# Turning q and k by 32 by 32 blocks on VectorE and transfers, with sums moved to GpSimd and to an adding transfer

## The chip, the cores and the metric

The kernel runs on one core of a Trainium2 chip. A core has TensorE (matmuls, with weight loads beside them), VectorE (DVE), ScalarE (ACT), GpSimd (POOL) and SyncE (SP, which here only issues transfers); ScalarE and GpSimd can issue transfers too. The metric is the device time of one execution in microseconds (us), less is better.

## The reference

Hashed attention over 4 batches, 8 heads, 768 tokens and 64 channels is followed by a two-layer network with a leaky activation.

```python
q_bits = (np.einsum('bhsd,dk->bhsk', q, proj) > 0)      # 6 bits; k_bits likewise
mask = q_bucket[:, :, :, None] == k_bucket[:, :, None, :]   # the bits as one number
scores = np.where(mask, scale * np.matmul(q, k.transpose(0, 1, 3, 2)), -1e9)
attn = softmax(scores)                                   # exp, sum, divide
x = (attn @ v), heads side by side                       # 3072 x 512
h = x @ w_in                                             # 512 x 2048
g = np.maximum(h, 0.0) + alpha * np.minimum(h, 0.0)
out = g @ w_out                                          # 2048 x 512
```

w_in and w_out come as 64-bit floats and are rounded to 32 bits in the kernel.

## The kernel before

The program tries `fast_path`; a flag that it computes decides whether `general_path` runs as well, and in the profiled execution it does not. `fast_path` has two parts: attention, and the two matrix products of the network, each of them done with seven half-size products in place of eight.

**Attention** works on 16 pairs of heads (`pi`), one after another. Of a pair, tokens lie on the partitions as they come from memory: token 6p + c is at partition p, slot c of the tile `nat`, whose row holds 64 channels of each of the two heads. Scores need channels on the partitions. `turn(pi, name)` makes them: six TensorE transposes of 128 by 128 into a PSUM tile, then one ScalarE copy into `tr` (q is scaled by a small constant there). The column order of `tr` is slot by slot. `hash_bits` multiplies `tr` with the projection and takes signs on ScalarE into `kb`; from there six small transfers on the SP queue bring the bits of q into `qb` and part of k's bits into place. `scores` goes through twelve cells (six tiles of 128 keys by two groups of 384 queries). A cell has, for each of the two heads, a bf16 matmul on the bits and an fp32 one on `tr`, which add up in PSUM, and one exponential on ScalarE over both heads into `pts[kc]`. `attend` multiplies with v, `totals` sums over keys with a matrix of ones, and `divide` finishes on VectorE and stores `x_s`.

The sum over six key tiles that `totals` needs is made on VectorE: `add_first` (tiles 0 and 1), `add_third` (tile 2), `add_last` (tiles 3 to 5, two additions), `add_total`. `magnitude` squares q and k in place on ScalarE, for the flag.

**Beside it**, two pieces of the weights are rounded in each iteration: `load_weight` (SP queue), `weight_abs` (two ScalarE passes), and `weight_clamp`, `weight_parts`, `weight_sum` on VectorE. For each of four groups of w_in, `weight_group` queues four more additions and a store into `w_in_s`; `weight_sums(2)` issues up to two of these additions an iteration.

**Order.** Most engine instructions go through `do`, which pins them behind what was written before on the same engine. Transfers without `do` are ordered by a planner that estimates when they are ready. PSUM has three two-bank tiles for scores, turns and sums. A tile's `tag` with `bufs=n` means that n tiles of this tag exist and that the next one waits until all users of the oldest are done.

The order of one iteration, cut to what matters here:

```python
scores(pi, ...); divide(pi - 1, weight_begin)   # with add_first(pi) inside
weight_sum(i); weight_group(i); load_weight(i + 3); weight_clamp(i + 1)
add_third(pi); add_last(pi); weight_parts(i + 1); weight_sum(i + 1)
weight_group(i + 1); load_weight(i + 4); add_total(pi); weight_sums(2)
hash_bits(pi + 1); turn(pi + 2, "q"); turn(pi + 2, "k")
attend(pi); totals(pi); weight_abs(i + 2); load(pi + 2, "v")
magnitude(pi, "q"); load(pi + 3, "q"); magnitude(pi, "k"); load(pi + 3, "k")
weight_abs(i + 3)
```

Pairs 0 and 1 are turned ahead of the loop.

Of the kernel before, what the change touches and what calls it, by code (L numbers as in the profile page):

```python
# [8 lines left out]
F32 = mybir.dt.float32  # L9
# [3 lines left out]
AF = mybir.ActivationFunctionType  # L13
ALU = mybir.AluOpType
# [393 lines left out]
def fast_path(  # L408
# [12 lines left out]
    nc = tc.nc  # L421
    P = 128
    B, H, S, D = q.shape
# [5 lines left out]
    NC = S // P  # L429
    NK = DM // P  # L430
    NF = DFF // P
    CH = 3
    NCH = NC // CH
    CW = CH * P
    HW2 = CW // 2
    SCALE = float(D) ** -0.5
    DOWN = 2.0 ** -20
# [5 lines left out]
    do = tc.keep_in_program_order  # L443
    PE, DVE, ACT, POOL = nc.tensor, nc.vector, nc.scalar, nc.gpsimd
# [32 lines left out]

    pts = [pool.tile([P, NCH, 2, CW + 1], F32, name=f"pt{i}", bufs=1) for i in range(NC)]

    nat, tr, bits = {}, {}, {}  # L480
    accp, accd, av, vsum, sums = {}, {}, {}, {}, {}

# [10 lines left out]
    def load_part(pi, name, cs, queue):  # L493
        b, hp = pairs[pi]
        src = {"q": q, "k": k}[name]
        if cs.start == 0:
            nat[name, pi] = pool.tile([P, NC, 2, D], F32, name=f"{name}n{pi}", tag=f"{name}n", bufs=3)
        for s in range(2):
            queue.dma_start(nat[name, pi][:, cs, s], src[b, 2 * hp + s].rearrange("(p c) d -> p c d", c=NC)[:, cs])

# [32 lines left out]
    def setup_alpha():  # L533
        ps = two_banks("alps")[:, 0, :NF]
        do(PE.transpose(ps, alpha16, ident[:NF, :NF]))
        do(DVE.tensor_copy(alpha, ps))
# [91 lines left out]
    def weight_group(i):  # L628

        i = order[i]  # L630
        if i >= HW:
            n, m = divmod(i - HW, 2)
            if m == 1:
                nc.sync.dma_start(w_out_r[:, :, n].rearrange("m p d -> p m d"), wst[HW + n])
            return
        n, m = divmod(i, 4)
        if m < 3:
            return
        w = wst[n]

        def one(to, a, op, c):
            do(DVE.tensor_tensor(w[:, to], w[:, a], w[:, c], op=op))

        def store():
            c, kk = divmod(n, 2)
            for ii in range(4):
                nc.sync.dma_start(w_in_s[4 * c + ii][:, :, kk], w[:, :, ii])


        for x in ((3, 5, 2), (5, 0, 5), (4, 3, 0), (6, 1, 4)):  # L650
            sums_due.append((one, (x[0], x[1], ALU.subtract, x[2])))
        sums_due.append((store, ()))
# [14 lines left out]
    def turn(pi, name, halves=BOTH, engine=None):  # L667
# [10 lines left out]
        else:  # L678
            do(ACT.activation(dst, ps[:, halves, :CW], AF.Copy, scale=DOWN if name == "q" else 1.0))

    def magnitude(pi, name):

        t = nat[name, pi].rearrange("p c h d -> p (c h d)")
        n = "qk".index(name)
        do(ACT.activation(t, t, AF.Square, accum_out=mags[:, n, pi : pi + 1]))

    def hash_bits(pi, halves=BOTH, engine=None):

        if halves.start == 0:
            bits["q", pi] = qbs[pi % 2]
            kb = pool.tile([P, 3 * CW], BF16, name=f"kb{pi}", tag="kb", bufs=1)
            bits["k", pi] = kb[:, :S]
            bits["raw", pi] = kb.rearrange("p (a w) -> p a w", w=CW)
        ps = {"k": two_banks(f"hs{pi}")}
        ps["q"] = psum_av.tile([P, 2, 512], F32, name=f"hsq{pi}", tag="av") if engine is DVE else ps["k"]
        for half in range(halves.start, halves.stop):
            for name in "qk" if engine is DVE else "kq":
                for s in range(2):  # L700
                    r, c = D * s, D * (s ^ half) + 32 * "kq".index(name)

                    for t, c in [("k", c)] + ([("q", c ^ D)] if engine is DVE and name == "q" else []):
                        do(PE.matmul(
                            ps[t][c : c + 32, half if t == "k" or engine is not DVE else 0, :CW], wh[r : r + D],
                            tr[name, pi][r : r + D, half * CW : (half + 1) * CW], start=True, stop=True,
                        ))
        if engine is None:
            raw = bits["raw", pi]
            do(ACT.activation(raw[:, 0:3:2], ps["k"][:, :, :CW], AF.Sign, bias=hb))  # L710
            for half in range(2):
                for s in range(2):
                    c = D * (s ^ half)
                    cols = slice(half * CW, (half + 1) * CW)
                    nc.sync.dma_start(bits["q", pi][D * s : D * s + 32, cols], raw[c + 32 : c + 64, 2 * half])
                    if half:
                        nc.sync.dma_start(bits["k", pi][D * s : D * s + D, cols], raw[c : c + D, 2])
            return
        for half in range(halves.start, halves.stop):
            cols = slice(half * CW, (half + 1) * CW)  # L720
            for s in range(2):
                c = D * (s ^ half ^ (engine is DVE)) + 32
                do(ACT.activation(
                    bits["q", pi][D * s : D * s + 32, cols], ps["q"][c : c + 32, 0 if engine is DVE else half, :CW], AF.Sign, bias=hb[c : c + 32],
                ))

            for to, c, n in [(0, 0, P)] if half == 0 else [(0, D, D), (D, 0, D)]:
                dst, src = bits["k", pi][to : to + n, cols], ps["k"][c : c + n, half, :CW]
                do(DVE.tensor_scalar(
                    dst, src, hb_k[c : c + n, 0:1], hb_k[c : c + n, 1:2], op0=ALU.is_gt, op1=ALU.subtract,  # L730
                ))


    def scores(pi, cells):
        for kc, g in cells:
            sc = two_banks(f"sc{pi}_{kc}_{g}")
            ks = slice(kc * P, (kc + 1) * P)
            qs = slice(g * CW, (g + 1) * CW)
            for what, first in ((bits, True), (tr, False)):
                for s in range(2):  # L740
                    r = slice(D * s, D * s + D)
                    do(PE.matmul(  # L742
                        sc[:, s, :CW], what["k", pi][r, ks], what["q", pi][r, qs], start=first, stop=not first,
                    ))
            do(ACT.activation(pts[kc][:, g, :, :CW], sc[:, :, :CW], AF.Exp, scale=SCALE / DOWN))  # L745


    def p(kc):
        return pts[kc].rearrange("p g s w -> p (g s) w")[:, :, :CW]

    def add_first(pi):
        accp[pi] = pool.tile([P, 2 * NCH, CW], F32, name=f"accp{pi}", tag="accp", bufs=1)
        do(DVE.tensor_tensor(accp[pi], p(0), p(1), op=ALU.add))  # L753

    def add_last(pi):
        accd[pi] = pool.tile([P, 2 * NCH, CW], F32, name=f"accd{pi}", tag="accd", bufs=1)
# [1 line left out]
        do(DVE.tensor_tensor(accd[pi], accd[pi], p(5), op=ALU.add))  # L758

    def add_third(pi):  # L760
        do(DVE.tensor_tensor(accp[pi], accp[pi], p(2), op=ALU.add))  # L761

    def add_total(pi):
        do(DVE.tensor_tensor(accd[pi], accd[pi], accp[pi], op=ALU.add))  # L764
# [375 lines left out]
    for pi in range(NPAIR):  # L1140
        i = 2 * pi

        def weight_begin():
            weight_clamp(i)
            weight_parts(i)
            add_first(pi)

        scores(pi, [c for c in CELLS if pi or c not in ahead])
        if pi:
            divide(pi - 1, weight_begin)  # L1150
        else:
            add_first(pi)
        weight_sum(i)
        weight_group(i)
        load_weight(i + 3)
        if pi == 0:
            weight_abs(1, DVE)
        weight_clamp(i + 1)
        add_third(pi)
        add_last(pi)  # L1160
        weight_parts(i + 1)
        weight_sum(i + 1)
        weight_group(i + 1)
        load_weight(i + 4)
        add_total(pi)
        weight_sums(2)
        if pi + 1 < NPAIR:
            hash_bits(pi + 1)
        if pi + 2 < NPAIR:
            turn(pi + 2, "q")  # L1170
            turn(pi + 2, "k")
        attend(pi)
        if pi + 1 == NPAIR:
            now = ff1(0, 0)
            now.step(1)
        totals(pi)
        if pi + 1 == NPAIR:
            now.step(5)
            divide(pi)
        else:  # L1180
            weight_abs(i + 2)
        if pi + 2 < NPAIR:
            load(pi + 2, "v")
        if pi in (9, 11, 15):
            load_w((9, 11, 15).index(pi))
        if pi in (9, 10, 12):
            load_x(0, *{9: (0,), 10: (2, 3), 12: (1,)}[pi])
        if 11 <= pi < 14 or pi == 15:
            sum_x(0, min(pi - 11, 3), DVE)
        if pi == 1:  # L1190
            setup_alpha()
        for name in "qk":
            magnitude(pi, name)
            if pi + 3 < NPAIR:
                load(pi + 3, name)
        if pi + 1 < NPAIR:
            weight_abs(i + 3)
# [97 lines left out]
```

## Time and profile before

| | us |
|---|---|
| three runs, median (lowest to highest) | 897.62 (896.51 to 897.95) |
| the profiled execution, its own time | 897.64 |
| span of its profile | 895.8 |
| TensorE busy | 884.2 (99%) |
| VectorE busy | 746.8 (83%) |
| ScalarE busy | 379.5 (42%) |
| GpSimd busy | 14.4 (2%) |
| attention: last store of `x_s` issued at | 347.3 |

The span is what the profiler saw of the core's instructions. Busy shares are means over the whole span; the two parts use the engines differently (from 60 to 310 us ScalarE is busy for 192.9 of 250 us, VectorE for 217.7, TensorE for 247.9). A group's line gives the source line, the engine, what is written from what, the count, then the busy time, the mean of one in ns, and the idle time ahead of it with what ended it. In the timeline a line begins with start and length in us. "SPq" is the issue of a transfer by SP.

### The profile page before, as it was taken

The numbers are of one execution on the slowest core, as the hardware profiler recorded it, in microseconds if no ns is written. First come the engines' busy times: TensorE is split into PE (matmuls) and PEld (weight loads), VectorE is DVE, ScalarE is ACT, GpSimd is POOL, SyncE is SP. The second block draws the span as 40 slices with busy tenths as digits, with TensorE's granted clock in tenths as the row PEclk, the third lists the DMA queues.
The fourth block names the chain that finished last, engine by engine and source line by source line (L and its number), as shares of the span: only waits on it lengthen the run. The fifth ranks groups of instructions, "written<-read, shape, count | busy, mean of one in ns | idle before, by whom it ended". The sixth has DMA issues, their size and how long they took to land.

```text
span 895.8 us, 15331 instructions
## 1 busy us (share of the span) xinstructions
PE 884.2 (99%) x5886; PEld 598.5 (67%) x5886; DVE 746.8 (83%) x1266; ACT 379.5 (42%) x668; POOL 14.4 (2%) x30
## 2 busy tenths in 40 slices
PE   9999999999999999999999999999999999999996
PEld 4544545555555545557997557997557998556996
DVE  5888888888989887899989678988668989768996
ACT  7877777788877762222112222112222111222111
POOL 1000000000000001120000000000000000000000
PEclk9999999999999999999999999999999999999998
DMA  8444575575685625587333435343525242430242
GB/s 235 139 143 129 151 232 153 149 229 173 204 281 163 202 74 185 181 296 289 141 113 107 163 111 166 107 147 88 178 88 192 95 159 80 157 116 0 95 143 72
DMA packets 126177, 137.22 MB, mean 153 GB/s; under 512 B 78976, under 2 KB 110224, under 8 KB 122512
## 3 DMA queue, kind: packets, MB, share of 16 engines
q1 hardware_dynamic: 121376, 126.59, 44.9%
q0 software_dynamic: 2304, 8.39, 2.6%
q10 hardware_dynamic: 2416, 1.18, 0.5%
q8 instruction: 48, 0.79, 0.3%
q14 instruction: 33, 0.27, 0.1%
HBM read 104.87 MB, written 28.31 MB: 149 GB/s over the span
## 4 chain that ended last, share of the span: by engine, by line
PE 84%; DVE 9%; issue 3%; ACT 2%; DMA 2%; SPq 0%; DVEq 0%; ACTq 0%
PE sc L742 12%; PE av L775 10%; PE f_0a L875 2%; PE z_4a L875 2%; PE z_7a L875 2%; PE z_3a L875 2%; PE z_6a L875 2%; PE z_5a L875 2%; PE f_4a L875 2%; PE f_3a L875 2%; PE f_2a L875 2%; PE f_1a L875 2%; PE z_2a L875 2%; PE f_5a L875 2%; DMA qb<-kb 2%
## 5 line engine op out<-in xcount | busy, mean ns | idle before, releaser
L745 ACT ACTIVATE pt<-sc 128x768 f32<-128x768 f32 x192 | 154.8, 812 | 53.5 <-PE sc L742 53.2
L742 PE MATMUL sc<-qT,kT 64*128 64x384 f32 x768 | 155.8, 483 | 0.0
L775 PE MATMUL av<-pt,vn 128*32 128x385 f32 (+1 forms) x1536 | 127.4, 486 | 0.0
L742 PEld LDWEIGHTS sc<-qT,kT 64*128 64x128 f32 x768 | 70.0, 187 | 40.9 <-issue 40.7
L775 PEld LDWEIGHTS av<-pt,vn 128*32 128x32 f32 x1536 | 48.7, 109 | 71.1 <-issue 70.5
L928 DVE TENSOR_TENSOR g<-g,g 128x384 f32<-128x384 f32 x128 | 68.4, 555 | 2.2
L742 PE MATMUL sc<-qb,kb 64*128 64x384 bf16 x384 | 66.5, 323 | 2.4 <-DMA qb<-kb 2.1
L992 DVE TENSOR_TENSOR gs<-g,gs 128x768 f32<-128x768 f32 x56 | 53.3, 952 | 1.0
L992 DVE TENSOR_TENSOR gs<-g 128x768 f32<-128x768 f32 x56 | 53.3, 951 | 0.0
L984 DVE TENSOR_TENSOR ws<-wl 128x512 f32<-128x512 f32 x56 | 38.5, 687 | 17.5 <-DMA wl<-w_out_s 15.9
L753 DVE TENSOR_TENSOR accp<-pt,pt 128x1536 f32<-128x1536 f32 x16 | 28.1, 1759 | 17.5 <-ACT pt L745 17.5
L924 DVE SCALAR_TENSOR_TENSOR g<-h,alpha 128x384 f32<-128x384 f32 x32 | 19.7, 616 | 25.1 <-ACT h L917 25.1
L742 PEld LDWEIGHTS <-kb 64*128 64x128 bf16 x384 | 20.9, 94 | 25.9 <-issue 4.3
L580 ACT ACTIVATE wr<-raw 128x512 int32<-128x512 uint32 x32 | 22.8, 712 | 17.2 <-issue 16.0
L758 DVE TENSOR_TENSOR accd<-accd,pt 128x1536 f32<-128x1536 f32 x16 | 28.1, 1759 | 2.0 <-ACT wr L580 0.5
L761 DVE TENSOR_TENSOR accp<-accp,pt 128x1536 f32<-128x1536 f32 x16 | 28.0, 1753 | 0.0
L757 DVE TENSOR_TENSOR accd<-pt,pt 128x1536 f32<-128x1536 f32 x16 | 28.0, 1752 | 0.0
L764 DVE TENSOR_TENSOR accd<-accd,accp 128x1536 f32<-128x1536 f32 x16 | 28.0, 1751 | 0.0
L805 DVE STREAM_TRANSPOSE st<-sm 128x192 f32<-128x192 f32 x32 | 10.3, 361 | 16.9 <-PE sm L789 16.9
L875 PE MATMUL f_0a<-x,wi 128*128 128x384 f32 x64 | 23.5, 489 | 0.0
L875 PE MATMUL f_4a<-x,wi 128*128 128x384 f32 x64 | 23.3, 486 | 0.0
L875 PE MATMUL f_1a<-x,wi 128*128 128x384 f32 x64 | 23.3, 486 | 0.0
(348 smaller groups left out, 1732.1 us busy)
## 6 DMA issues: line engine op xcount, KB each, us to landing
wi<-w_in_s SPq DMA_DIRECT2D x32, 896.0 KB, 4.7
wl<-w_out_s SPq DMA_DIRECT2D x16, 1024.0 KB, 4.8
wl<-w_out_r SPq DMA_DIRECT2D x12, 1024.0 KB, 4.9
raw<-in_moe_w_out_dram SPq DMA_DIRECT2D x16, 512.0 KB, 3.9
raw<-in_moe_w_in_dram SPq DMA_DIRECT2D x16, 512.0 KB, 4.0
w_in_s<-wsi SPq DMA_DIRECT2D x16, 448.0 KB, 5.8
vn<-in_v_dram SPq DMA_DIRECT2D x16, 384.0 KB, 4.2
x_s<-x SPq DMA_DIRECT2D x16, 384.0 KB, 2.8
```

The costliest lines, as they stand in the source:

```text
L742: do(PE.matmul(sc[:, s, :CW], what["k", pi][r, ks], what["q", pi][r, qs], start=first, stop=not first,))
L745: do(ACT.activation(pts[kc][:, g, :, :CW], sc[:, :, :CW], AF.Exp, scale=SCALE / DOWN))
L753: do(DVE.tensor_tensor(accp[pi], p(0), p(1), op=ALU.add))
L757: do(DVE.tensor_tensor(accd[pi], p(3), p(4), op=ALU.add))
L758: do(DVE.tensor_tensor(accd[pi], accd[pi], p(5), op=ALU.add))
L761: do(DVE.tensor_tensor(accp[pi], accp[pi], p(2), op=ALU.add))
L764: do(DVE.tensor_tensor(accd[pi], accd[pi], accp[pi], op=ALU.add))
L775: do(PE.matmul(av[pi][D * s + t : D * s + t + 32, g, :w], nat["v", pi][:, s, kc * D + t : kc * D + t + 32], pts[kc][:, g, s, :w], start=(k ...
L875: do(PE.matmul(self.ps[bank], self.left(left, k), self.right(right, k), start=start and k == 0, stop=k == self.nk - 1, skip_group_check=no ...
L928: do(DVE.tensor_tensor(new_g(b, to)[:, i], g_m[b, x][:, i], g_m[b, y][:, i], op=ALU.subtract))
L984: do(DVE.tensor_tensor(t, w2[b, n, x], w2[b, n, y], op=op))
L992: do(DVE.tensor_tensor(t, g2[b, n, x], g2[b, n, y], op=ALU.subtract))
```

## The change

- q and k of pairs 2 to 15 are no longer turned by `turn`. `turn_blocks` lets VectorE transpose all 32 by 32 blocks of `nat` at once into a tile of tag "tb" (one buffer for both names), and sixteen transfers on the SP queue, each of 32 partitions by 192 floats, put the blocks at their place in `tr`. k comes first, then q. The columns of `tr` are then in token order; `columns` picks a tile's columns out of `tr` and of the bits with a step of six elements. `scale_q` scales q on ScalarE.
- `nat` has two buffers instead of three for q and k, and `magnitude` runs two pairs ahead.
- The six transfers of `hash_bits` go to ScalarE's queue and are pinned in its order.
- The four additions of a w_in group run on GpSimd.
- From pair 1 on, half of `add_third` is done by an adding transfer on GpSimd's queue, issued in `add_first`.

```diff
-            nat[name, pi] = pool.tile(..., tag=f"{name}n", bufs=3)
+            nat[name, pi] = pool.tile(..., tag=f"{name}n", bufs=2 if name in WITH_DVE else 3)
...
-            do(DVE.tensor_tensor(w[:, to], w[:, a], w[:, c], op=op))
+            do(POOL.tensor_tensor(w[:, to], w[:, a], w[:, c], op=op))
...
+    def turn_blocks(pi, name):
+        t = pool.tile([P, 4, 32, NC], F32, name=f"{name}B{pi}", tag="tb", bufs=1)
+        do(DVE.transpose(t.rearrange("p b i c -> p b c i"), nat[name, pi].rearrange("p c h (e d) -> p (h e) c d", d=32)))
+        w = NC * 32
+        tr[name, pi] = dst = pool.tile([P, S], F32, name=f"{name}T{pi}", tag=f"{name}T")
+        for a in range(4):
+            for b in range(4):
+                nc.sync.dma_start(
+                    dst[32 * b : 32 * b + 32, a * w : (a + 1) * w],
+                    t[32 * a : 32 * a + 32, b].rearrange("p i c -> p (i c)"),
+                )
+        by_blocks.add((name, pi))
+
+    def scale_q(pi):
+        if ("q", pi) in by_blocks:
+            do(ACT.activation(tr["q", pi], tr["q", pi], AF.Copy, scale=DOWN))
+
+    def columns(what, name, pi, r, c0, c1):
+        t = what[name, pi][r]
+        if (name, pi) not in by_blocks:
+            return t[:, c0 * P : c1 * P]
+        t = t.rearrange("p (t c) -> p c t", c=NC)[:, c0:c1]
+        return t[:, 0] if c1 - c0 == 1 else t
...
-                    nc.sync.dma_start(bits["q", pi][D * s : D * s + 32, cols], raw[c + 32 : c + 64, 2 * half])
+                    do(nc.scalar.dma_start(bits["q", pi][D * s : D * s + 32, cols], raw[c + 32 : c + 64, 2 * half]))
                     if half:
-                        nc.sync.dma_start(bits["k", pi][D * s : D * s + D, cols], raw[c : c + D, 2])
+                        do(nc.scalar.dma_start(bits["k", pi][D * s : D * s + D, cols], raw[c : c + D, 2]))
...
-                        sc[:, s, :CW], what["k", pi][r, ks], what["q", pi][r, qs], start=first, stop=not first,
+                        sc[:, s, :CW], columns(what, "k", pi, r, kc, kc + 1),
+                        columns(what, "q", pi, r, CH * g, CH * (g + 1)), start=first, stop=not first,
...
         do(DVE.tensor_tensor(accp[pi], p(0), p(1), op=ALU.add))
+        if pi:
+            nc.gpsimd.dma_start(accp[pi][:, 2:], p(2)[:, 2:], accum_op=ALU.add)
...
-        do(DVE.tensor_tensor(accp[pi], accp[pi], p(2), op=ALU.add))
+        n = 2 if pi else 4
+        do(DVE.tensor_tensor(accp[pi][:, :n], accp[pi][:, :n], p(2)[:, :n], op=ALU.add))
...
             hash_bits(pi + 1)
+        if pi == 0:
+            for name in WITH_DVE:
+                magnitude(0, name)
         if pi + 2 < NPAIR:
-            turn(pi + 2, "q")
-            turn(pi + 2, "k")
+            turn_blocks(pi + 2, "k")
+            turn_blocks(pi + 2, "q")
         attend(pi)
...
+        scale_q(pi + 2)
         for name in "qk":
-            magnitude(pi, name)
+            for n in [1, 2] if pi == 0 and name in WITH_DVE else [pi + 2 * (name in WITH_DVE)]:
+                if n < NPAIR:
+                    magnitude(n, name)
```

More of the change, by code (lines that the diff above doesn't have):

```diff
@@ L478, in fast_path @@
     pts = [pool.tile([P, NCH, 2, CW + 1], F32, name=f"pt{i}", bufs=1) for i in range(NC)]
+    WITH_DVE = "qk"
     nat, tr, bits = {}, {}, {}
@@ L496, in load_part @@
         if cs.start == 0:
-            nat[name, pi] = pool.tile([P, NC, 2, D], F32, name=f"{name}n{pi}", tag=f"{name}n", bufs=3)
+            nat[name, pi] = pool.tile([P, NC, 2, D], F32, name=f"{name}n{pi}", tag=f"{name}n", bufs=2 if name in WITH_DVE else 3)
         for s in range(2):
@@ L679, in turn @@
             do(ACT.activation(dst, ps[:, halves, :CW], AF.Copy, scale=DOWN if name == "q" else 1.0))
+    def turn_blocks(pi, name):
[10 more added lines that the diff above has]
+        by_blocks.add((name, pi))
+    by_blocks = set()
+    def scale_q(pi):
[7 more added lines that the diff above has]
+        return t[:, 0] if c1 - c0 == 1 else t
     def magnitude(pi, name):
@@ L736, in scores @@
             sc = two_banks(f"sc{pi}_{kc}_{g}")
-            ks = slice(kc * P, (kc + 1) * P)
-            qs = slice(g * CW, (g + 1) * CW)
             for what, first in ((bits, True), (tr, False)):
```

## The prediction

> **What bounds the kernel now.** I read the page's busy shares and clock first, then the groups by line, then the timeline of single engines over one head pair, since a share says nothing of order.
>
> ```profile
> PE 884.2 (99%) x5886; PEld 598.5 (67%) x5886; DVE 746.8 (83%) x1266; ACT 379.5 (42%) x668; POOL 14.4 (2%) x30
> ...
> PEclk9999999999999999999999999999999999999998
> ```
>
> TensorE is busy throughout at full clock, so every microsecond taken off it alone could be won. The stage that the change touches is the attention part, sixteen pairs up to about 350 us. Its groups of TensorE turns:
>
> ```profile
> L674 PE MATMUL tp_q<-ident,qn 128*128 128x128 f32 x96 | 14.5, 287 | 0.0
> L674 PE MATMUL tp_k<-ident,kn 128*128 128x128 f32 x96 | 13.6, 277 | 0.0
> ```
>
> Matmuls overlap, so I take the cost from the timeline: the first tp_q starts at 167.82 and the next stage (av) at 169.28, thus 1.46 us a pair. Next ScalarE's timeline, one pair:
>
> ```profile
> 168.05 0.90 ACT L710 ACTIVATE kb<-hs,hb 128x768 bf16<-128x768 f32 x1
> ...
> 174.26 0.73 ACT L580 ACTIVATE wr<-raw 128x512 int32<-128x512 uint32 x1 [1.09 <-issue]
> 174.88 0.70 ACT L584 ACTIVATE wx<-raw 128x512 f32<-128x512 f32 x1
> 178.92 9.70 ACT L745 ACTIVATE pt<-sc 128x768 f32<-128x768 f32 x12 [3.34 <-PE sc L742]
> 188.65 0.90 ACT L710 ACTIVATE kb<-hs,hb 128x768 bf16<-128x768 f32 x1
> ```
>
> The Sign (L710) follows a pair's last exponential at once; its starts mark the pairs. From the first (22.59) to the fifteenth (314.27) are 14 intervals in 291.7 us, **20.83 us a pair**. ScalarE waits 3.34 us for scores before the next pair's twelve exponentials. VectorE and SP in the same pair:
>
> ```profile
> 170.63 1.76 DVE L758 TENSOR_TENSOR accd<-accd,pt 128x1536 f32<-128x1536 f32 x1
> ...
> 174.10 1.75 DVE L764 TENSOR_TENSOR accd<-accd,accp 128x1536 f32<-128x1536 f32 x1
> ```
> ```profile
> 168.97 1.85 SPq L715 DMA_DIRECT2D qb<-kb  x3
> ```
> ```profile
> L715 SPq DMA_DIRECT2D qb<-kb x60: 511/585/1282, 23.6 to 320.9; - x60
> ...
> DMA to landing us min/median/max: 1.8/2.4/5.4
> ```
>
> VectorE is only 7.85 us behind: the last exponential ends at 168.00, add_total (L764) at 175.85. SP takes 0.62 us from issue to issue (three in 1.85) for a transfer of 32 rows of 768 bytes that lands after 2.4 us. The new transfers have just this shape.
>
> [...]
>
> **The change part by part.** Fourteen pairs (2 to 15) are turned the new way, in iterations 0 to 13.
>
> *Removed.* TensorE 1.46 us a pair, in all 20.4 us; ScalarE's two copies, 0.81 us each; VectorE's sixteen w_in adds of 0.69 us, 11.0 us in all, and half of each later add_third, 0.88 us.
>
> *Added on a serial path.* This decides. All engine instructions concerned are pinned in program order, so a wait holds everything behind it.
> 1. k's block turn stands on VectorE behind add_total, and q's directly behind k's. Both write a tile of tag "tb" with bufs=1, so q's turn waits until all sixteen of k's transfers have read it. Behind it wait divide and the next pair's sums.
> 2. scale_q stands on ScalarE behind weight_abs and ahead of the squares, weight_abs(i+3) and **the next pair's exponentials**. It waits for q's sixteen transfers.
> 3. add_total needs this pair's last exponential. So one pair's exponentials, both rounds of transfers, and the next pair's exponentials form a chain.
>
> From one last exponential to the next:
> - to the end of add_total: 7.85 - 0.88 = 6.97
> - k's turn: 0.97 (L816, a transpose of as many elements)
> - k's transfers: 15 x 0.62 + 2.4 = 11.7
> - q's turn and transfers: 0.97 + 11.7
> - scale_q: 0.85 (as an L685 square)
> - both squares: 1.79 (150.14 to 151.93)
> - weight_abs(i+3): 1.31 (153.02 to 154.33)
> - twelve exponentials: 9.70
>
> Sum **46.0 us**, against 20.83. Outside the transfers it is already 22.6.
>
> *Unknowns on it.* Restart: TensorE finishes its work some 9 us after E (E: a pair's last exponential) and then idles over 20 us[...]. A scores cell takes 0.81 us, as long as an exponential; [...] I take 1.5. Strided scores: k and q are now read in steps of 24 bytes, their bits 12. Bounds: nothing, or a cell at half speed, 0.8 us x 12 = 9.7 us a pair. In the timeline a cell's fp32 matmuls start 0.16 us after its bf16 ones and fill the other 0.64 in two passes, half the bf16 pace, so I expect the bf16 pass alone to suffer, 0.08 of its 0.16 us: 1.0 us a pair. The strided weight loads overlap matmuls (a step of 8 bytes costs 196 against 190 ns in the z products); I count them in that bound. Together **48.5 us a pair**.
>
> *Moved, with cover.* Six bit transfers go to ScalarE: 6 x 0.6 = 3.6 us behind the Sign, inside its new wait for scale_q, so nothing; uncovered they'd be 3.6 us a pair. SP gains 32 x 0.62 = 19.8 us and loses 3.7; its other transfers (q, k, v, raw, x_s, w_in_s) take some 6 us, so 26 of 48.5 us: not the bound, though whatever is queued between the new ones delays them, 0 to 5 us a pair. In four iterations it can be w_in_s's four stores (4.5 us). The w_in adds run on GpSimd while VectorE waits: nothing[...]. The adding transfer starts after add_first (about E - 4.7), passes POOL's queue, and at the 6.8 us of POOL's own loads lands at E + 2, before add_total at E + 5.2: nothing; if its tile is tracked whole, add_third waits some 3 us. Shorter buffers for q and k cost once: pair 2's load waits for magnitude(0), behind the Sign (0.9), six issues (3.6) and two squares (1.8), so it starts at E + 6.3 and lands at E + 11.9, 4.9 late; iteration 0 has two squares more, 1.8. Together 6.7 us.
>
> *Sum.* 14 x 48.5 = 679.0, less 291.7: +387.3. With 6.7 and 1.0 for pair 15's strided scores: +395. The profiled execution took 897.64 (span 895.8), the median of three runs is 897.62: **1292 us**. TensorE's 20.4 us are saved where nobody waits.
>
> **The rivals.** *Cheaper issue.* SP issues a plain full-width load in 0.33 us and the output's pieces in about 0.47. At 0.35 a round is 4 us shorter, the pair 8.1: 1292 - 14 x 8.1 = 1179. For it speaks that L715's cost is not explained by its bytes; against it, 60 equal transfers never went under 0.51. *Strided reads at half speed.* A cell goes from 0.81 to 1.6 us and TensorE paces the exponentials: 9.7 for 1.0, 1292 + 14 x 8.7 = 1414. *Only VectorE is held.* If scale_q did not stand before the exponentials, VectorE alone would set the pair: busy 217.7 of 250 us, or 18.1 a pair, less 0.9 and 0.8 plus 1.9 for the turns, plus one round of 11.7 and hand-offs: 30.2, so 897.6 + 14 x 9.4 = 1029. The order in the code speaks against it. *Faster.* Turns hidden altogether, TensorE still the bound: 897.6 - 20.4 = 877. It decides below 20.83 us a pair; with the sum's 22.6 us outside the transfers even free transfers miss that, so ScalarE and VectorE would both have to run past the waits. That the turns don't leave TensorE is excluded by the diff.
>
> **How the numbers follow.** Both rounds on the path near 0.6 us an issue: 0.68, own range 1210 to 1380. Cheaper issue 0.11, strided reads at half speed 0.12, VectorE alone 0.06, turns hidden 0.02, a tie by accident 0.01. A measurement of this kernel can tell about 0.2% (1.8 us) from no change. The range of 8 in 10 runs from the cheap end to the strided end: 1180 to 1420. Faster 0.02, same 0.01, slower 0.97.
>
> **What would show it.** Right: exponentials of pairs 1 to 14 behind a wait of some 27 us for scale_q, this behind q's transfers; some 12 us of idle VectorE before each q turn; Sign starts about 48 us apart; attention ending near 745 us, later stages as long as now; low clock digits in it. Wrong: q's turn close behind k's, exponentials ahead of scale_q, or issues of 0.3 us.

## The result, and the profile after

| | us |
|---|---|
| before, median of the runs beside it | 897.68 (896.51 to 897.95) |
| after, median of four runs | 1374.15 (1373.63 to 1375.16) |
| ratio after to before | 1.531 (95% interval 1.529 to 1.534) |
| span of the profile after | 1372.6 |
| last store of `x_s` issued at | 823.6 (before: 347.3) |

The kernel takes half as long again. The last store of `x_s` moved by 476.3 us, which is the whole difference: from there to the end of the span it is 549.0 us after and 548.5 before. So only the attention part is to be read.

From the page of after come first the busy shares and the granted clock, then the share of each engine in the chain of work that ended last, then four groups (out<-in, count | busy us, mean ns of one | idle us before it, and what ended it):

```profile
PE 1050.5 (77%) x5718; PEld 638.6 (47%) x5718; DVE 778.0 (57%) x1278; ACT 365.9 (27%) x654; POOL 58.6 (4%) x61
...
PEclk9588687786786886876867899999999999999999
...
PE 57%; SPq 18%; DVE 9%; ACT 5%; DMA 5%; issue 2%; ACTq 1%; DVEq 0%
...
L768 PE MATMUL sc<-qb,kb 64*128 64x384 bf16 x384 | 131.6, 646 | 312.4 <-ACT pt L772 184.8
L768 PE MATMUL sc<-qT,kT 64*128 64x384 f32 x768 | 285.8, 815 | 0.0
...
L684 DVE STREAM_TRANSPOSE qB<-qn 128x768 f32<-128x768 f32 x14 | 21.5, 1534 | 165.3 <-DMA kT<-kB 165.3
L699 ACT ACTIVATE qT<-qT 128x768 f32<-128x768 f32 x14 | 11.8, 842 | 358.3 <-DMA qT<-qB 358.3
```

No engine is near full, and the issue of transfers by SP (SPq) is 18% of the chain, 247 us. The two waits of the prediction are there, fourteen times each: q's turn waits 165.3 / 14 = 11.8 us for k's transfers, `scale_q` (L699) 358.3 / 14 = 25.6 us for q's. TensorE has 168 instructions fewer and is busy 166 us **longer**: a matmul of the scores takes 815 ns (fp32) and 646 ns (bf16), where the page of before has 483 and 323:

```profile
L742 PE MATMUL sc<-qT,kT 64*128 64x384 f32 x768 | 155.8, 483 | 0.0
L742 PE MATMUL sc<-qb,kb 64*128 64x384 bf16 x384 | 66.5, 323 | 2.4 <-DMA qb<-kb 2.1
```

One pair, in ScalarE's timeline (start us, length us; in brackets the idle time before it and what ended it):

```profile
293.14 0.90 ACT L738 ACTIVATE kb<-hs,hb 128x768 bf16<-128x768 f32 x1
...
324.11 0.84 ACT L699 ACTIVATE qT<-qT 128x768 f32<-128x768 f32 x1 [24.24 <-DMA qT<-qB]
...
327.60 2.19 ACT L772 ACTIVATE pt<-sc 128x768 f32<-128x768 f32 x3
330.53 0.81 ACT L772 ACTIVATE pt<-sc 128x768 f32<-128x768 f32 x1 [0.74 <-PE sc L768]
332.39 0.81 ACT L772 ACTIVATE pt<-sc 128x768 f32<-128x768 f32 x1 [1.06 <-PE sc L768]
...
346.39 0.90 ACT L738 ACTIVATE kb<-hs,hb 128x768 bf16<-128x768 f32 x1
```

VectorE and SP in the same pair:

```profile
296.52 1.75 DVE L794 TENSOR_TENSOR accd<-accd,accp 128x1536 f32<-128x1536 f32 x1
298.19 1.62 DVE L684 STREAM_TRANSPOSE kB<-kn 128x768 f32<-128x768 f32 x1
311.30 1.53 DVE L684 STREAM_TRANSPOSE qB<-qn 128x768 f32<-128x768 f32 x1 [11.48 <-DMA kT<-kB]
```
```profile
299.88 10.08 SPq L689 DMA_DIRECT2D kT<-kB  x16
...
312.85 10.02 SPq L689 DMA_DIRECT2D qT<-qB  x16
```

Read from top to bottom by time, this is one thread: last exponential (ends 293.02), add_total, k's turn, sixteen issues, landing, q's turn, sixteen issues, landing, `scale_q`, squares, `weight_abs`, the next exponentials. Each step begins where the one before it ends. The Sign starts lie 53.2 to 55.0 us apart, in the mean of 14 intervals (22.04 to 778.27) **54.0 us**; the prediction had 48.5. What it didn't have is the last stretch: behind the third exponential each one waits for TensorE, and they come every 1.87 us instead of every 0.81.

### The profile page after: what moved, and what is told of

It reads as the page before. It is cut to its first block, busy times and chain, and to the rows that moved or that the text cites. A ratio compares the mean times of both kernels' runs of the same rounds, so it can differ in the third digit from the quotient of the medians.

```text
span 1372.6 us, 15577 instructions
## 1 busy us (share of the span) xinstructions
PE 1050.5 (77%) x5718; PEld 638.6 (47%) x5718; DVE 778.0 (57%) x1278; ACT 365.9 (27%) x654; POOL 58.6 (4%) x61
## 4 chain that ended last, share of the span: by engine, by line
PE 57%; SPq 18%; DVE 9%; ACT 5%; DMA 5%; issue 2%; ACTq 1%; DVEq 0%
SPq L689 18%; PE sc L768 18%; DMA qT<-qB 2%; DMA kT<-kB 2%; DVE accd L794 2%; DVE kB L684 2%; DVE qB L684 2%; PE z_4a L905 2%; PE f_0a L905 2%; PE z_3a L905 2%; PE z_5a L905 2%; PE z_7a L905 2%; PE z_6a L905 2%; PE f_3a L905 2%; PE f_1a L905 2%
## 5 line engine op out<-in xcount | busy, mean ns | idle before, releaser
L768 PE MATMUL sc<-qb,kb 64*128 64x384 bf16 x384 | 131.6, 646 | 312.4 <-ACT pt L772 184.8
L768 PE MATMUL sc<-qT,kT 64*128 64x384 f32 x768 | 285.8, 815 | 0.0
L768 PEld LDWEIGHTS <-kb 64*128 64x128 bf16 x384 | 29.6, 120 | 397.8 <-issue 260.4
L772 ACT ACTIVATE pt<-sc 128x768 f32<-128x768 f32 x192 | 152.0, 809 | 136.6 <-PE sc L768 136.6
L768 PEld LDWEIGHTS sc<-qT,kT 64*128 64x128 f32 x768 | 121.9, 293 | 100.7 <-issue 100.3
L684 DVE STREAM_TRANSPOSE qB<-qn 128x768 f32<-128x768 f32 x14 | 21.5, 1534 | 165.3 <-DMA kT<-kB 165.3
L699 ACT ACTIVATE qT<-qT 128x768 f32<-128x768 f32 x14 | 11.8, 842 | 358.3 <-DMA qT<-qB 358.3
L782 POOL DMA_DIRECT2D accp<-pt x15 | 18.1, 1209 | 725.9 <-DVE x L852 380.9
L643 POOL TENSOR_TENSOR wsi<-wsi 128x512 f32<-128x512 f32 x16 | 27.9, 1746 | 27.4 <-DVE wsi L625 26.7
L684 DVE STREAM_TRANSPOSE kB<-kn 128x768 f32<-128x768 f32 x14 | 22.8, 1627 | 5.2 <-DMA kn<-in_k_dram 5.2
```

The source lines that it names most:

```text
L684: do(DVE.transpose(t.rearrange("p b i c -> p b c i"), nat[name, pi].rearrange("p c h (e d) -> p (h e) c d", d=32)))
L768: do(PE.matmul(sc[:, s, :CW], columns(what, "k", pi, r, kc, kc + 1), columns(what, "q", pi, r, CH * g, CH * (g + 1)), start=first, stop=no ...
```

## The experiments

Each variant was timed beside the kernel before. "Sign spacing" is the time between the starts of two Signs, a pair's period. e1 to e4 ask for the price of each link of the chain, e8 splits the price of the stepped reads, and the others ask what is left once the chain is broken or the turns stay on TensorE.

### e1_strided: the stepped reads alone

The kernel before, with TensorE's turns; only the column order of `tr` is changed for pairs 2 to 15.

```diff
-            do(ACT.activation(dst, ps[:, halves, :CW], AF.Copy, scale=...))
+            dst = tr[name, pi].rearrange("p (t h c) -> p h c t", h=NCH, c=CH)[:, halves] if pi > 1 else dst
+            src = ps[:, halves, :CW].rearrange("p h (c t) -> p h c t", c=CH) if pi > 1 else ps[:, halves, :CW]
+            do(ACT.activation(dst, src, AF.Copy, scale=...))
...
-                        sc[:, s, :CW], what["k", pi][r, ks], what["q", pi][r, qs], start=first, stop=not first,
+                        sc[:, s, :CW], columns(what, "k", pi, r, kc, kc + 1),
+                        columns(what, "q", pi, r, CH * g, CH * (g + 1)), start=first, stop=not first,
```

> The kernel before, with one thing added: for pairs 2 to 15 ScalarE's copy writes the turned q and k in token order, so that scores reads both, and their bits, in steps of six elements, as after does. TensorE still turns; no new transfer or wait. Theory (the strided reads are a cost of their own, in the new profile a cell takes 1.87 us at half and at full clock): 12 x (1.87 - 0.81) = 12.7 us a pair, 14 pairs, 897.7 + 178 = 1075 us. Rival (the long cells of after come from TensorE's restarts at half clock): cells stay at 0.81 us and the time at 898 to 905 us.

Measured: **1072.83 us**, ratio 1.195 (1.193 to 1.197). Its score groups:

```profile
L750 PE MATMUL sc<-qT,kT 64*128 64x384 f32 x768 | 290.0, 807 | 0.0
...
L750 PE MATMUL sc<-qb,kb 64*128 64x384 bf16 x384 | 137.4, 642 | 0.2 <-DVE kb L739 0.2
```

The means are those of after, at a mean clock of 0.998. So the long cells in after come from the stepped reads and not from a slow restart: this rival falls. The price is (1072.83 - 897.45) / 14 = 12.5 us a pair, and its cause is visible in a cell: 12 x (1.87 - 0.81) = 12.7. ScalarE's copies, which write in steps here, are longer too (q's 1.55 us in the mean for 0.81, k's 1.68 for 0.81), but TensorE is busy for 249.95 of the 250 us from 60 to 310, so they are not on the path.

### e8_strided_k: which operand pays

e1 with only k, whose tiles are TensorE's weights, in token order; q, which is streamed, is contiguous.

```diff
-        if pi < 2:
+        if pi < 2 or name == "q":
             return t[:, c0 * P : c1 * P]
...
```

> e1 with only k (the stationary operand, loaded as weights) in token order and read in steps; q and its bits stay contiguous. Theory (the streamed operand's reads are what slows a cell; weight loads run beside matmuls): 897 to 905 us. Rival (the stepped weight loads set the cell): up to 1073 us as in e1.

Measured: **914.76 us**, ratio 1.019 (1.017 to 1.020).

```profile
L750 PE MATMUL sc<-qT,kT 64*128 64x384 f32 x768 | 167.8, 513 | 0.0
L750 PEld LDWEIGHTS sc<-qT,kT 64*128 64x128 f32 x768 | 100.1, 291 | 32.5 <-issue 32.3
```

A stepped weight load takes 291 ns (187 before), yet the kernel is only 1.2 us a pair longer, since most of a load lies beside matmuls (the fp32 loads take 30.1 us more in all, 100.1 for 70.0, the kernel 17.1). In TensorE's timeline the cells start 0.87 us apart instead of 0.81, 0.7 us a pair; beside that TensorE waits 8.3 us in all for k's bits, 0.6 us a pair, and why these come later was not tested. The expectation of at most 905 us was missed. The other 11.3 of e1's 12.5 us go to the streamed operand by difference; no run stepped q alone.

### e4_natural: the change without stepped reads

Key tiles and query tiles are now 128 consecutive tokens, so the columns that the block turn leaves are read without a step; v is loaded and the output stored in that order (v with two transfers instead of one), and so are q and k of pairs 0 and 1, which TensorE turns. The chain stays.

```diff
-        if (name, pi) not in by_blocks:
-            return t[:, c0 * P : c1 * P]
-        t = t.rearrange("p (t c) -> p c t", c=NC)[:, c0:c1]
-        return t[:, 0] if c1 - c0 == 1 else t
+        return t[:, c0 * P : c1 * P]
...
-            nc.sync.dma_start(t, src[b, 2 * hp : 2 * hp + 2].rearrange("h (p c) d -> p h (c d)", c=NC))
+            for s in range(2):
+                nc.sync.dma_start(
+                    t[:, s].rearrange("p (c d) -> p c d", d=D), src[b, 2 * hp + s].rearrange("(c p) d -> p c d", c=NC)
+                )
...
```

> After, with v loaded (and pairs 0 and 1 turned, and the output written) in natural token order, so that a tile of 128 keys or a group of queries is a run of neighbouring columns and scores reads without steps; the block turns and all transfers stay. Theory: cells go back to 0.81 us, plus some 1.5 us a pair for restarts at half clock: twelve exponentials in 11.2 instead of 18.7 us, 1374 - 14 x 7.5 = 1269 us. Rival (the slow cells are the slow clock): cells stay above 1.6 us through most of a pair, above 1340 us.

Measured: **1286.82 us**, ratio 1.433 (1.431 to 1.436); Sign spacing 48.5 us in the mean. ScalarE's timeline:

```profile
304.69 2.19 ACT L772 ACTIVATE pt<-sc 128x768 f32<-128x768 f32 x3
307.35 0.81 ACT L772 ACTIVATE pt<-sc 128x768 f32<-128x768 f32 x1 [0.47 <-PE sc L768]
308.95 0.81 ACT L772 ACTIVATE pt<-sc 128x768 f32<-128x768 f32 x1 [0.79 <-PE sc L768]
310.29 5.66 ACT L772 ACTIVATE pt<-sc 128x768 f32<-128x768 f32 x7 [0.52 <-PE sc L768]
```

Twelve exponentials take 315.95 - 304.69 = 11.26 us, 1.6 more than the 9.70 of before; the gaps all stand behind the first cells that TensorE computes. After has the same gaps, 0.47 and 0.79 us, in pair 1, whose scores read without steps: from 66.00 to 70.71 us its cells start 1.55 to 1.60 us apart, and the granted clock is 0.50 from 66 to 70; behind that they start 0.81 apart, and the clock is 1.00 from 72 to 76. So I read e4's 1.6 us as the restart, seen alone, near its predicted 1.5. The exponentials are 7.3 us shorter than in after, but in the 13 intervals that have stepped cells in after the period falls only from 53.9 to 48.0 us. The rest lies behind the last exponential: add_total ends 323.46 - 315.95 = 7.5 us after it here, 5.25 in after. GpSimd's sums and VectorE's timeline show why:

```profile
313.31 3.21 POOL L646 TENSOR_TENSOR wsi<-wsi 128x512 f32<-128x512 f32 x2 [0.72 <-DVE wsi L628]
```
```profile
315.31 2.82 DVE L786 TENSOR_TENSOR accd<-pt,pt 128x1536 f32<-128x1536 f32 x1
```

Beside the sums, a VectorE addition that takes 1.76 us alone takes 2.82. In the 13 pairs the distance is 5.5 to 5.6 us in five, 6.4 and 6.6 in two, and 6.7 to 8.9 in the six that have sums there; after has them too, but with its slow cells VectorE has time to spare and stays at 5.2 to 5.6. In the mean it is 6.9 against 5.3, and 13 x 1.6 = 21 us is near the 18 that e4 stands above its expectation.

### e3_tb2: two buffers for the block turns

```diff
-        t = pool.tile([P, 4, 32, NC], F32, name=f"{name}B{pi}", tag="tb", bufs=1)
+        t = pool.tile([P, 4, 32, NC], F32, name=f"{name}B{pi}", tag="tb", bufs=2)
```

> After, with two buffers for the block-turned tile, so that q's turn no longer waits for k's transfers. Theory: VectorE's stall of 11.5 us a pair goes, but SP still issues 32 transfers one behind another, 32 x 0.62 + 1.8 = 21.8 us from k's turn, where the two rounds with the turn between took 24.4; 2.6 us a pair, 1374 - 36 = 1338 us. Rival (VectorE's stall is what sets the time): 1374 - 14 x 11.5 = 1213 us.

Measured: **1332.83 us**, ratio 1.484 (1.482 to 1.487). SP's timeline shows why the second buffer is worth 41 us and not 160:

```profile
284.83 10.08 SPq L689 DMA_DIRECT2D kT<-kB  x16
295.00 10.03 SPq L689 DMA_DIRECT2D qT<-qB  x16
```

q's turn no longer waits, and the rounds stand back to back. What goes is one landing, one turn and the hand-off; both issue times stay, since one queue issues them. The rounds are bound by issues, as expected.

### e2_late: nothing of the next pair ahead of the exponentials

```diff
-        scale_q(pi + 2)
-        for name in "qk":
-            for n in [1, 2] if pi == 0 and name in WITH_DVE else [pi + 2 * (name in WITH_DVE)]:
-                if n < NPAIR:
-                    magnitude(n, name)
+        for name in "qk":
+            if pi == 0:
+                magnitude(1, name)
...
         scores(pi, [c for c in CELLS if pi or c not in ahead])
+        if 0 < pi < NPAIR - 1:
+            scale_q(pi + 1)
+            for name in "qk":
+                magnitude(pi + 1, name)
```

> After, with scale_q and both squares moved on ScalarE from ahead of the next pair's exponentials to behind them. Theory (transfers and exponentials form one serial chain because ScalarE is held): the chain breaks; what is left is TensorE with strided cells, 12 x 1.87 + 0.8 + 7.8 + 0.8 = 31.8 us a pair, or both rounds up to the scaled q, which the next hash needs, 32.0 us after the last exponential; some 33 us a pair, 1374 - 14 x 21 = 1080 us. Rival (only VectorE's stall and SP's issues set the time): 1340 to 1374 us.

Measured: **1139.04 us**, ratio 1.269 (1.266 to 1.272). Moving three ScalarE instructions saves 235 us, which shows the chain: the period falls from 54.0 to 37.4 us. It missed its expectation by 59 us. What is late next, from VectorE's timeline, SP's and ScalarE's:

```profile
304.05 1.53 DVE L684 STREAM_TRANSPOSE qB<-qn 128x768 f32<-128x768 f32 x1 [14.42 <-DMA kT<-kB]
```
```profile
290.79 11.37 SPq L689 DMA_DIRECT2D kT<-kB  x16
```
```profile
308.17 0.81 ACT L772 ACTIVATE pt<-sc 128x768 f32<-128x768 f32 x1 [3.82 <-PE sc L768]
```

VectorE still stands 14.4 us for `tb`, and behind it `divide`'s first transpose, which frees the PSUM tile of the sums. Scores need this tile, so the exponentials stop in the middle of a pair. That is the rival "only VectorE is held", at 37 us where the prediction put 30 without the stepped cells.

### e5_all3, e10_unheld_nat, e11_unheld: the chain broken in several ways

e5 joins e2, e3 and e4. e10 takes e3 and e4 with `scale_q` alone moved behind the exponentials, the squares left early. e11 is e10 with the stepped reads kept. The edit common to e10 and e11, beside bufs=2:

```diff
-        scale_q(pi + 2)
...
         scores(pi, [c for c in CELLS if pi or c not in ahead])
+        if pi:
+            scale_q(pi + 1)
```

> After with the edits of e2, e3 and e4 together: the ScalarE work behind the exponentials, two buffers for the turned tile, natural token order. Theory (three prices on one chain, then SP's issues as the next bound): SP has 32 x 0.63 = 20.2 us for the blocks and some 6 us for q, k, v, raw, x_s and w_in_s, 26.2 us a pair, 897.5 + 14 x (26.2 - 20.8) = 973 us. Rival (with the waits and steps gone TensorE is the bound again, 1.46 us a pair shorter): 877 us. Rival (a stall not yet seen, as VectorE against GpSimd): above 1020 us.

> e5, but only scale_q stands behind the exponentials; the squares stay where after has them, since with two turned tiles they wait for q's turn alone. Theory (e5 lost its time because late squares freed the q and k tiles late, so loads and turns formed a loop of their own; without it SP's issues bound): 26.2 us a pair, 973 us. Rival (SP's issues and landings cost more in this order than their sum, or another loop is left): above 1040 us.

> After with two turned tiles and scale_q behind the exponentials; the reads in steps stay. Theory: neither VectorE nor ScalarE is held, TensorE with stepped cells bounds, 12 x 1.87 + 0.8 + 7.8 + 0.8 = 31.8 us a pair, 897.5 + 14 x 11 = 1051 us, near e1's 1073 less 14 x 1.46. Rival (the serial chain is something else than these two waits): 1139 us as e2, or more.

Measured: e5 **1103.75**, ratio 1.231 (1.228 to 1.233); e10 **1109.58**, 1.237 (1.234 to 1.240); e11 **1114.81**, 1.242 (1.239 to 1.245). All three missed by 64 to 137 us. For e5 I had counted what SP issues (26.2 us a pair) and taken the largest sum for the period. e10 shows the reason, in VectorE's timeline, SP's and TensorE's:

```profile
228.71 1.52 DVE L687 STREAM_TRANSPOSE kB<-kn 128x768 f32<-128x768 f32 x1
```
```profile
231.15 1.48 SPq L503 DMA_DIRECT2D qn<-in_q_dram  x2
232.75 5.48 SPq L503 DMA_DIRECT2D kn<-in_k_dram  x2
...
240.11 13.30 SPq L692 DMA_DIRECT2D kT<-kB  x16
```
```profile
196.28 1.02 PE L732 MATMUL hs<-qT,wh 64*32 64x384 f32 x2 [10.63 <-ACT qT L702]
```

k's turn ends at 230.23, but SP first issues the next loads of q and k and two more transfers, and begins with k's blocks at 240.11; 32 issues later q lands, ScalarE scales it, the hash can run, and only then `attend`, the sums, the next exponentials and the next turns. The last line is the hash of the round before: TensorE stands 10.6 us for the scaled q, with `attend` queued behind. So, as the trace reads, the loop was still closed, through TensorE's order instead of ScalarE's, with some 35 us around it (Sign spacing 35.2 us in e5, 35.7 in e10, in the mean). No run opened this link alone. The theory for e10, that the late squares held the loads in e5, falls with it: both come out within 6 us.

e11 stands 5 us above e10 although its cells cost 12 us a pair more. TensorE is busy there for 365 of the 380 us from 100 to 480 and sets the period; with fast cells, in e10, it is busy for 247 and the loop sets it, at nearly the same length. With two bounds of some 35 us, taking one away brings next to nothing.

### e7_dram, e12_dram2: fewer issues

e5 with the six bit transfers back on SP, and sixteen block transfers replaced by four stores to a scratch tile in DRAM and one load. e12 adds the order: q first, the hash behind two of `attend`'s six key tiles, only the squares behind the Sign.

```diff
-            for b in range(4):
-                nc.sync.dma_start(
-                    dst[32 * b : 32 * b + 32, a * w : (a + 1) * w],
-                    t[32 * a : 32 * a + 32, b].rearrange("p i c -> p (i c)"),
-                )
+            nc.sync.dma_start(
+                hop[:, :, a].rearrange("b d x -> d b x"), t[32 * a : 32 * a + 32].rearrange("p b i c -> p b (i c)")
+            )
+        nc.sync.dma_start(dst, hop.rearrange("b d a x -> (b d) (a x)"))
...
```

> e5 with the sixteen transfers of a name replaced by five through memory (four stores of 32 partitions into a scratch tensor ordered by channel, one plain load of 128 rows), and the bit transfers back on SP. SP's share falls to about 10 x 0.6 + 3.7 + 6 = 16 us a pair. Theory (turning by blocks as such can pay once its transfers are few and nobody is held by them): TensorE 20.83 - 1.46 = 19.4 us a pair, VectorE 18.1 - 0.9 - 0.8 + 3.2 = 19.6, so some 19.6 us and 897.5 - 14 x 1.2 = 880 us. Rival (doubled traffic and the longer way delay other transfers, or VectorE's waits add up): 900 us or more.

> e7 with its remaining waits spread: the hash of the next pair stands after two of the six key tiles of attend, so that q's way through memory has 2.6 us more; q is turned ahead of k; the squares stand behind the next pair's Sign. Theory (e7 loses some 4 us a pair where TensorE waits for the scaled q before the hash, 3.4 us at 212.4): that wait goes, and a pair takes 19.6 to 21 us, 880 to 900 us. Rival (traffic at 0.88 of the transfer engines makes every landing late, so the wait moves to the bits): 910 us or more.

Measured: e7 **954.46**, ratio 1.063 (1.061 to 1.065); e12 **960.08**, 1.069 (1.066 to 1.073). Five transfers for sixteen, with the bits' issues off ScalarE, save 149 us against e5, 10.7 a pair, so the issues were a large part of the loop. It doesn't reach the kernel before. TensorE's waits in e7 and then in e12 (us in all, times, longest):

```profile
PE hs L733 <- ACT qT L703: 26.0, 14, 3.6
PE sc L769 <- DMA qb<-kb: 22.9, 11, 6.2
```
```profile
PE sc L769 <- DMA qb<-kb: 51.8, 17, 7.9
```

e12 took the hash's wait away and the bits' wait grew by 29 us. Both kernels keep the DMA engines busy for 0.89 and 0.87 of the time from 60 to 350 us, against 0.63 in before from 60 to 310, and the landing of q's bits, 2.4 us in the median before, takes 3.7 and 4.1 us. That the fuller engines lengthen the landing would fit, but k's bits land in 2.7 us in both, 3.5 before, and no run tested it alone; why q's bits come late stays open.

### e6_others, e9_pooladd: the rest of the change, with TensorE's turns

e6 takes the other parts of the change alone (GpSimd's sums, the adding transfer, bits on ScalarE); in e9 the bits are back on SP.

```diff
-WITH_DVE = "qk"
+WITH_DVE = ""
...
-            turn_blocks(pi + 2, "k")
-            turn_blocks(pi + 2, "q")
+            turn(pi + 2, "q")
+            turn(pi + 2, "k")
```

> After with q and k turned by TensorE again; what stays of the change is the w_in sums on GpSimd, the adding transfer, and the six bit transfers on ScalarE's queue. Theory (none of these is on the path): 894 to 902 us. Rival (GpSimd blocking VectorE, the adding transfer, or ScalarE's 4 us of issues belong to the loss): 910 us or more.

> e6 with the six bit transfers back on SP: of the change only the w_in sums on GpSimd and the adding transfer are left. Theory (e6's 10 us come from ScalarE, which stands in its order behind transfers that it issues itself): 896 to 900 us. Rival (they come from GpSimd and VectorE blocking each other or from the adding transfer): 904 us or more.

Measured: e6 **907.65**, ratio 1.012 (1.010 to 1.014); e9 **919.19**, 1.024 (1.023 to 1.026). e6 came out 10 us slower instead of level. My theory after it, that the loss goes when ScalarE no longer issues the bits, falls with e9, where it issues none and the time rises.

e6's Sign spacing is 20.2 to 20.8 us in all pairs but four of them, which have 23.8, 24.2, 23.8 and 24.1; over the 14 intervals that makes its 10 us. These are the pairs in which `w_in_s` is stored; the adding transfer, which every pair from the second on has, costs nothing in the others. One of them, in SP's timeline and in ScalarE's:

```profile
104.63 5.56 SPq L648 DMA_DIRECT2D w_in_s<-wsi  x4
```
```profile
105.52 3.11 ACTq L743 DMA_DIRECT2D qb<-kb  x3
...
113.40 0.50 ACTq L745 DMA_DIRECT2D kb<-kb  x1
113.95 0.81 ACT L680 ACTIVATE qT<-tp_q 128x768 f32<-128x768 f32 x1 [8.46 <-DMA kb<-kb]
```

and SP's timeline in before:

```profile
106.49 1.85 SPq L715 DMA_DIRECT2D qb<-kb  x3
...
117.80 4.72 SPq L647 DMA_DIRECT2D w_in_s<-wsi  x4
```

The sums on GpSimd end at 104.61 and release the stores at once, ahead of the bits; in before the stores come after them. In e6 the bits' six issues then take from 105.52 to 113.90 on ScalarE (in after they take 4.5 us, 294.07 to 298.53, with a single issue of SP beside them), and the scaled copy and the exponentials wait behind. In e9 SP issues the four stores at 105.71 and the bits at 111.34, and the intervals behind the four groups of stores are 24.3, 25.2, 25.7 and 27.5 us. TensorE's longest waits in e6 and then in e9 say the same (us in all, times, longest):

```profile
PE sc L768 <- ACT pt L772: 7.4, 4, 2.0
```
```profile
PE sc L768 <- DMA qb<-kb: 14.4, 7, 3.6
```

So the two kernels pay in the same pairs: in e6 scores wait for exponentials that stand behind ScalarE's slow issues, in e9 for bits that stand behind SP's stores. VectorE is stretched in these pairs too (below), but in e6 none of TensorE's waits in the loop is for its sums. No run held the stores back.

## Why the prediction was right, and by how much it was off

**The chain: right.** The direction, the two waits and their order are those of the prediction, and e2 shows that the place of `scale_q` and the squares makes the chain. One pair against its steps, from one last exponential's end to the next (293.02 to 346.27):

| step | predicted | measured |
|---|---|---|
| to the end of add_total | 6.97 | 5.25 |
| two turns | 1.94 | 3.07 |
| two rounds of transfers | 23.4 | 22.77 |
| scale_q, squares, weight_abs | 3.95 | 3.58 |
| twelve exponentials, restart and steps included | 12.2 | 18.58 |
| sum | 48.5 | 53.25 |

**The rounds: right**, 11.49 and 11.28 us for 11.7. An issue took 588 ns in the median and a landing 1.8 us instead of 2.4. The rival "cheaper issue" falls: none of 448 went under 507 ns.

**Strided scores: the mis-sized term.** I put 1.0 us a pair, on the argument that only the bf16 pass would suffer because the fp32 matmuls take the data at half its pace (0.64 us in two passes for 0.16). In the pair above the twelve exponentials take 18.58 us, 7.3 more than in e4 without steps. Where TensorE alone paces, in e1, it is 12.5, more than my upper bound of 9.7. Of the 0.81 us cell, the bf16 part went from 0.16 to 0.51 us and the fp32 part from 0.64 to 1.35. The price, 2.3 times a cell (1.87 us for 0.81), is only in the runs. The rival "strided reads at half speed", at 0.12, named what happened, and its 1414 lies nearer to the 1374 measured than my 1292; it was too high because it added a restart and kept the long tail. So the chain was foreseen, but that the time still lies inside 1180 to 1420, and by 6 us inside my own 1210 to 1380, is owed to the width of these ranges and not to my price for the steps: in this part it is luck.

**Restart: right in size, absent in place.** e4 has it at 1.6 us; the 1.5 was an estimate of mine that no trace had shown. In after it vanishes in the stepped pairs, since a stepped cell takes as long at a granted clock of 0.50 as at 1.00. The table of windows of after (window, then busy us of PE, PEld, DVE, ACT, POOL, then PEclk) covers the idle stretch with the first two of a pair's exponentials that wait for scores, and a later stretch:

```profile
311.00:333.00 22.00, 6.61 (x22) 3.10 (x24) 6.03 (x15) 7.10 (x12) 0.00 (x0) 0.50 0.28 72
337.00:346.00 9.00, 9.00 (x44) 3.43 (x40) 3.45 (x2) 3.78 (x5) 2.75 (x2) 1.00 0.46 104
```

At clocks of 0.50 and 1.00 the exponentials come 1.87 us apart in both. What lowers the clock around the idle stretch, and when, was not tested.

**The tail: counted too long.** I took VectorE's lag of before and added the restart to it. But VectorE catches up while the exponentials wait: with fast cells, in e4's five quiet pairs, add_total ends 5.5 us behind the last exponential, which fits 6.97 less the restart's 1.5. In after, with cells of 1.87 us, it is 5.25. So the slow cells shortened this link little; what they hid is the stretching by GpSimd's sums, up to 8.9 us in e4.

**The turns: off.** I took 0.97 us from a transpose of as many elements that writes contiguously. This one writes in steps of 24 bytes and takes 1.53 to 1.62. That the steps are the reason was not tested, and the other transpose reads a repeated source as well.

**The sum, and the shorter buffers: right.** The first interval holds the exponentials of pair 1, which TensorE turned and scores reads without steps; it is 55.0 us all the same, and 48.5 + 6.7 is 55.2. So the 6.7 us for the shorter buffers are there: k's first turn waits 5.17 us for its load, and the two more squares take 1.65. The other 13 intervals are 53.9 us in the mean, 5.4 above 48.5, together 71 us. From the last Sign to the last store of `x_s` it is 45.4 us, before 33.1: 12 us more where I had 1.0, again the steps of pair 15 (e4 has 32.8). 71 and 11 make the 82 us between 1292 and 1374.

**Moved with cover: right only in this kernel, and in part for another reason.** In after the bits' issues lie inside ScalarE's wait for q, as predicted. The adding transfers and 12 of GpSimd's 16 sums do not lie in such a wait: they run beside the exponentials (in the pair above from 335.37 to 339.83), where VectorE, though stretched (its half of `add_third` takes 1.78 us there, 0.95 in the median), still waits 3.88 us for an exponential that a slow cell holds up. Without the chain and the slow cells the moved parts cost 10 us (e6). A sum took 1.75 us on GpSimd in the mean, 0.69 on VectorE before. The stores of `w_in_s` that pass ahead of the bits are the piece that I had named for SP's queue and not priced for ScalarE's.

**Turns off TensorE: no gain anywhere.** No kernel here without them beats the one before; the closest is e7, at 954. Only in e11, where TensorE sets the period, would its 1.46 us a pair count, and there the steps cost far more.

## What to carry to other kernels

For every instruction that is moved into an order written out by hand, first follow what it waits for and what stands behind it, around the loop until it closes; in the four runs here where such a loop was left, expectations from sums of busy time were off by 59 to 137 us. A burst of small transfers costs its count times the issue time before anyone can use the result (16 x 0.6 us here), so a second buffer helps little while one queue issues them (3 us a pair in e3). If a new layout makes the operand that TensorE streams non-contiguous, price that first, by itself: it came to 11.3 us a pair by difference (e1 less e8), and it was the second largest term here and looked like a detail.

## What the runs showed of the hardware

- With both operands of the scores read in steps of 24 bytes (fp32) and 12 bytes (bf16), a cell took 1.87 us instead of 0.81, **at granted clocks of 0.50 and 1.00 alike** (after); the same steps on the weights alone made an fp32 load 291 ns instead of 187 and a cell 0.87 us (e8).
- In two places a queue's issues took longer while another queue issued: three bit transfers took 3.1 us to issue beside SP's stores in e6, 1.8 in after; SP's two loads of k took 5.5 us beside ScalarE's issues in e10, 1.3 in after. SP's four stores took no longer for it (5.6 us in e6, 5.5 in e9, where ScalarE issued none beside them). What slows an issue was not tested.
- Beside GpSimd's two-input adds VectorE's two-input instructions took longer (2.82 us for 1.76 in e4), and one add took 1.28 to 2.74 us itself in after. GpSimd's and VectorE's timeline of e6; the second VectorE line is behind the sums, in the same pair:

```profile
101.18 3.43 POOL L643 TENSOR_TENSOR wsi<-wsi 128x512 f32<-128x512 f32 x2
```
```profile
101.73 1.73 DVE L622 SCALAR_TENSOR_TENSOR wx<-raw,wx 128x512 uint32<-128x512 uint32 x1
...
110.53 0.69 DVE L622 SCALAR_TENSOR_TENSOR wx<-raw,wx 128x512 uint32<-128x512 uint32 x1
```

Beside the sums the same instruction took two and a half times as long, 1.73 us for 0.69.
